# DeltaNet and a maxout FFN on one core: the last prologue links and the first four FFN pieces in program order, and a reordered second group

## The chip, the cores and the metric

The kernel runs on one core of a Trainium2 chip. The metric is the device time of one launch in microseconds (us). A core has five engines with queues of their own: TensorE (PE, with its weight loads PEld), VectorE (DVE), ScalarE (ACT), GpSimd (POOL) and SyncE (SP), which here only issues DMA transfers.

## The reference

There are two stages. The first is a delta-rule recurrence over 768 steps for 4 batches x 8 heads with head size 48, the second a maxout FFN over 3072 tokens.

```python
B, H, S, D = q.shape                       # 4, 8, 768, 48
k_n = k / (np.linalg.norm(k, axis=-1, keepdims=True) + 1e-06)
for t in range(S):
    y[:, :, t] = np.einsum('bhd,bhde->bhe', q[:, :, t], state)
    v_old = np.einsum('bhde,bhd->bhe', state, kt)
    state = state + bt[:, :, :, None] * np.einsum('bhd,bhe->bhde', kt, vt - v_old)

x = y.transpose(0, 2, 1, 3).reshape(B * S, H * D)          # (3072, 384)
h = np.maximum(np.maximum(x @ w1, x @ w2), x @ w3)         # 768 columns
out = h @ w_out                                            # (3072, 384)
```

All is float32. The FFN weights arrive as 64-bit numbers and are put together from their two halves on the chip.

## The kernel before

The sequence is cut into 12 chunks of 64 steps. A chunk has two units (two of the four batches each), so there are 24 units, and two chunks make a group: six groups, and a group's 512 tokens are also what one call of `ffn` takes. Within a chunk the steps depend on one another through a triangular system, which is solved first: `gram` multiplies keys with keys (tile `at`) and with queries (tile `pt`), `to_dram` and `blocks` bring the diagonal blocks of `at` into another layout through DRAM, and `solve(m)` substitutes for the two chunks of group m on DVE, column by column (L519 multiplies, L523 subtracts). For the first two groups (`FINE = 2`) the blocks have 16 columns, and `halves_z` and `halves_u` join two of them to one of 32 (tiles p_e, p_f). `join_z` and `join_u` (p_z, p_j) join the blocks of 32 to the full system `ut`, with T1, the transposed first block, from `turn_t1` (L569, L571). `old_k` and `old_q` read the state (p_k, p_q), `new` makes the update u (p_u), `step` adds it to the state `st` (p_s, L732), `to_y` makes the output (p_y) and `to_x` turns it into the FFN's input `xt` (p_x).

`ffn(m)` is a generator: each piece is one product with one of the three weights (p_h, three 128x128 blocks) and a copy on ACT or a maximum on DVE (L831, L833), and it ends with four pieces for the output (p_o). For m = 0, pieces 0 to 8 take the first 256 tokens and pieces 9 to 17 the other 256, for half of the hidden columns; so the first FFN can start when only chunk 0 is done. p_h and p_o share two PSUM buffers (`ps_ffn`), all products of the recurrence share three (`ps_two`).

Between two pieces the kernel writes the links of the next group. A table gives, for each piece, letters with a chunk or unit: z and j are the joins, e and f the halves, d is T1, k, q, u, s, y, x the recurrence, t and g the turns and Grams of a unit, L and N loads of keys and queries in blocks for a later turn. The loop of group 0 takes the links of group 1 from `EARLY_LINKS`, and also what is left of chunk 1 from `FIRST` (there T and P are the turns and Grams of queries alone). The loops of groups 1 to 4 use `LINKS` for the group after.

In the prologue and in the loops of groups 1 to 5, all engines follow the program (`manual_schedule()`). In the loop of group 0, only TensorE does; a planner puts the work of DVE, ACT, POOL and SP in the order that its own costs give.

The FFN weights come in 24 pieces of 384 KB through five buffers (`fetch`, L192). `some(conv, 1)` puts one of them together: ACT L211 and L220, POOL L215, DVE L230 and L234, POOL L238; a piece's DVE part is written one step after its ACT part, and each of its two temporary tiles has two buffers. `solve(1)` keeps its two tiles in the space of `wo_sb`, which the last six weight pieces fill later.

In the loops from group 1 on, `turn` is `turn_blocks`: DVE transposes (L385) from tiles `turned`, which `load_blocks` fills with eight key loads on SP and eight query loads on POOL (L369).

Of the kernel before, what the change touches and what calls it, by code (L numbers as in the profile page):

```python
# [21 lines left out]
def kernel(  # L22
# [31 lines left out]
    nc = tc.nc  # L54
# [70 lines left out]
    def load_q(n, queues=one_queue):  # L125
        load(q, qpad[n % NQ], n, queues)
# [61 lines left out]
    def fetch(queue=nc.scalar):  # L188
        if fetched[0] < len(pieces):
            _, src, (a, b) = pieces[fetched[0]]  # L190
            st = work.tile([128, 2 * 384], U32, name="w_bits", bufs=5)
            queue.dma_start(  # L192
                out=st.rearrange("p (a b) -> p a b", a=a), in_=src
            )
            staged.append(st)
            fetched[0] += 1
# [133 lines left out]
    def turn(n, parts=(0, 1), copy=nc.scalar.copy):  # L330

        if n not in kqts:
            kqts[n] = work.tile([128, NP, 2, 2, C], FP32, name="kqt", bufs=6)
        kqt = kqts[n]
        p_t = ps_two("p_t")
        for i in parts:
            src = (kpad[n % NK], qpad[n % NQ])[i]
            for j in range(NP):
                nc.tensor.transpose(
                    p_t[:, i, j * 128 : (j + 1) * 128],  # L340
                    src[:, 2 * j : 2 * j + 2],
                    ident,
                )
        some = slice(parts[0], parts[-1] + 1)
        copy(  # L345
            kqt.rearrange("p j b i t -> p i (j b) t")[:, some],
            p_t.rearrange("p i (x t) -> p i x t", t=C)[:, some],
        )
# [51 lines left out]
    def gram(n, parts=(0, 1), queues=one_queue, copy=nc.scalar.copy, later=False):  # L400
        kqt, g = kqts[n], n % 2
        p_g = ps_two("p_g")

        whole = len(parts) == 2 and not g
        for j in range(NP):
            for par in range(2):
                for bb in range(2):
                    kq = kqt[dims(par), j, bb ^ g]
                    for i in (0,) if whole else parts:
                        c0 = j * 128 + i * C  # L410
                        nc.tensor.matmul(  # L411
                            p_g[
                                rows(bb ^ (g * i)), par, c0 : c0 + C * (1 + whole)
                            ],
                            kq[:, 0],
                            kq if whole else kq[:, i],
                        )
        p_v = p_g.rearrange("p two (j i t) -> p two j i t", j=NP, i=2)
        if 1 in parts:
            pt = pts[n] = square("pt")  # L420
            if later:
                copy(by_par(pt), p_v[:, :, :, 1])
            else:
                masked(pt, p_v[:, :, :, 1])
        if 0 not in parts:
            return
        at = ats[n] = square("at")
        copy(by_par(at), p_v[:, :, :, 0])  # L428
        if queues:
            to_dram(n, queues)  # L430

    def to_dram(n, queues=one_queue):


        m, cc, g, at = n // 4, n % 4 // 2, n % 2, ats[n]
        if m not in at_d:
            at_d[m] = dram.tile([2, C, B, H, C], FP32, name="at_d")
        for bb in range(2):
            queues[bb].dma_start(
                out=at_d[m][cc, :, 2 * bb + g].rearrange("j h i -> j (h i)"),  # L440
                in_=at[rows(bb)].rearrange("p h i -> p (h i)"),
            )
# [123 lines left out]
    def turn_t1(c):  # L566

        t, u_t = t1[c % NU], ut[c % NU]
        nc.vector.transpose(out=t[:, 0], in_=u_t[:, 0, :, 0:BL])  # L569
        for bb in range(2):  # L570
            nc.vector.transpose(  # L571
                out=t[block(1 - bb), 1], in_=u_t[block(bb), 1, :, 0:BL]
            )
# [28 lines left out]
    def halves_z(c):  # L602
        if c not in fine:
            halves_t(c)
        at = [ats[2 * c + g] for g in range(2)]
        second = ut[c % NU].rearrange("p g h (f two x) -> p g h f two x", two=2, x=HB)
        for hs, p_v, copy in heads_of(c, "p_e", BL):
            for i, h in enumerate(hs):
                for bb, g in TILES:
                    r = rows(bb)  # L610
                    nc.tensor.matmul(
                        p_v[rows(bb ^ g), g, i], at[g][r, h], second[r, g, h, :, 1]
                    )
            copy(zs[c % NU][:, :, span(hs)], p_v)
# [7 lines left out]
    def halves_u(c):  # L622
        t, z = fine.pop(c), zs[c % NU]
        for hs, p_v, _ in heads_of(c, "p_f", BL):
            for i, h in enumerate(hs):
                for bb, g in TILES:
                    r = rows(bb ^ g)
                    nc.tensor.matmul(p_v[rows(bb), g, i], t[g][r, h], z[r, g, h])
            for f in (0, 1):
                for bb in range(2):  # L630
                    r = block(bb, f, HB)
                    negated(
                        bb,
                        ut[c % NU][r, :, span(hs), BL * f + HB : BL * (f + 1)],
                        p_v[r, :, :, HB * f : HB * (f + 1)],
                    )
        turn_t1(c)

    def join_z(c):
        at = [ats.pop(2 * c + g) for g in range(2)]  # L640
# [109 lines left out]
    def to_x(c):  # L750
        m, cc = divmod(c, 2)
        if m not in xts:
            xts[m] = work.tile([128, KT, TOK], FP32, name="xt")
        y_f = yts.pop(c).rearrange("p g h d -> p g (h d)")
        p_x = ps_two("p_x")
        for g in range(2):
            for t in range(KT):
                nc.tensor.transpose(
                    p_x[:, g, t * 128 : (t + 1) * 128],
                    y_f[:, g, t::KT],  # L760
                    ident,
                )
        xt = xts[m][:, :, cc * 256 : (cc + 1) * 256].rearrange(
            "p t (g x) -> p g t x", g=2
        )
        copied(c, xt, p_x[:, :, 0 : KT * 128].rearrange("p g (t x) -> p g t x", t=KT))
# [96 lines left out]
    def some(gen, n):  # L863
        for _ in range(n):
            if next(gen, gen) is gen:
                break
# [56 lines left out]
        masked(pts[n], by_par(pts[n]))  # L923
    for c in range(2):
        scale(c, nrm_0[:, c])
    some(conv, 2)
    for n in range(2):
        fetch(nc.sync)
    to_dram(6)
    to_dram(7)  # L930
    halves_z(0)
    some(conv, 1)
    fetch(nc.sync)
    blocks(1)
    halves_u(0)
    fetch(nc.sync)
    join_z(0)
    some(conv, 1)
    fetch(nc.sync)
# [7 lines left out]
    fetch(nc.sync)  # L947
    load_q(2)
    to_y(0)
    halves_z(1)  # L950
    some(conv, 1)
    fetch(nc.sync)
    to_x(0)
    load_q(3)
    load_q(4)
    load_v(2)
    some(conv, 1)
    fetch(nc.sync)
    solving = solve(1)
    by_hand.close()  # L960
    tc.no_sync_barrier()

    LINKS = {
# [4 lines left out]
    }  # L971
    EARLY_LINKS = {
# [3 lines left out]
    }  # L976

    FIRST = {
        0: "f1 s0 T2", 1: "z1 k1 P2 T3", 2: "j1", 3: "P3 q1", 4: "u1 T4",
        5: "y1", 6: "s1 T5 P4", 7: "x1 T6", 8: "P5 T7", 12: "P6", 14: "P7",  # L980
    }


# [3 lines left out]
    )  # L987
    MADE = dict(V=load_v, p=prep_sums, P=prep_values)
    UNIT = dict(t=turn, g=gram, K=load_k, L=load_blocks)
    OF_KEYS = dict(T=lambda n: turn(n, (1,)), P=lambda n: gram(n, (1,)))  # L990

    def links(m, names):
        for name in names.split():
# [18 lines left out]
                load_q(n + 3)  # L1012


    by_hand = ExitStack()
    by_hand.enter_context(tc.manual_schedule(engines={mybir.EngineType.PE}))
    for i, _ in enumerate(ffn(0)):
        if i > 2:
            some(conv, 1)
            fetch(nc.sync)  # L1020
        queries(FIRST.get(i, ""))
        links(1, EARLY_LINKS.get(i, ""))
        if 2 <= i < 9:
            some(solving, 3)
        if i == 4:
            load_v(3)
        if 5 <= i < 9:
            load_k(3 + i)
        if i in (8, 9):
            prep(i - 6)  # L1030
        if i == 12:
            load_q(11)
        if i in (15, 18):
            load_v(4 + i // 18)
        if i in (18, 20):
            prep(4 + i // 20)
        if i == 19:
            blocks(2)
        if i == 21:
            solving = solve(2)  # L1040
            some(solving, 1)
        if 21 <= i < 29:
            some(solving, 4)
        if i in (27, 28):
            load_blocks(i - 15)
# [52 lines left out]
```

## Time and profile before

| | us |
|---|---|
| median of 6 runs | 592.57 (590.66 to 595.69) |
| profiled execution | 590.66 |
| its span | 588.9 |
| PE busy | 538.7 (91%) |
| DVE busy | 343.7 (58%) |
| ACT busy | 140.4 (24%) |
| POOL busy | 119.8 (20%) |
| p_h, 702 matmuls (L823) | 301.6, mean 575 ns |
| p_o, 288 matmuls (L847) | 94.6, mean 487 ns |

The page also gives the span in 40 equal slices of 14.7 us, the busy share in tenths:

```
PE   5468468987999999999989999999999999999997
DVE  1658969388399363699653799663997432201110
PEclk9555859999999999999999999999999999999999
```

PEclk is the clock that TensorE was granted, in tenths of its full speed. The first FFN piece starts at 61 us, right after p_x of chunk 0. A line of an order in time has start, length, engine, line, operation and tiles; in brackets stand the time for which the engine had been idle and what ended it. "issue" is idle time for which the profile shows no reason.

### The profile page before, as it was taken

The numbers are of one execution on the slowest core, as the hardware profiler recorded it, in microseconds if no ns is written. First come the engines' busy times: TensorE is split into PE (matmuls) and PEld (weight loads), VectorE is DVE, ScalarE is ACT, GpSimd is POOL, SyncE is SP. The second block draws the span as 40 slices with busy tenths as digits, with TensorE's granted clock in tenths as the row PEclk, the third lists the DMA queues.
The fourth block names the chain that finished last, engine by engine and source line by source line (L and its number), as shares of the span: only waits on it lengthen the run. The fifth ranks groups of instructions, "written<-read, shape, count | busy, mean of one in ns | idle before, by whom it ended". The sixth has DMA issues, their size and how long they took to land.

```text
span 588.9 us, 18726 instructions
## 1 busy us (share of the span) xinstructions
PE 538.7 (91%) x8106; PEld 317.3 (54%) x8106; DVE 343.7 (58%) x778; ACT 140.4 (24%) x274; POOL 119.8 (20%) x209
## 2 busy tenths in 40 slices
PE   5468468987999999999989999999999999999997
PEld 5337356775555555555545555555455455554444
DVE  1658969388399363699653799663997432201110
ACT  3336635345211212111121121221211111010000
POOL 6024534127400243001913003800001000000000
PEclk9555859999999999999999999999999999999999
DMA  9998974655611563264664464843743102210002
GB/s 156 155 178 233 205 137 132 109 159 122 116 30 24 110 139 85 58 138 106 162 135 89 92 100 105 197 97 69 122 106 75 30 2 55 68 40 1 0 0 53
DMA packets 159505, 58.76 MB, mean 100 GB/s; under 512 B 141184, under 2 KB 153280, under 8 KB 159424
## 3 DMA queue, kind: packets, MB, share of 16 engines
q1 hardware_dynamic: 150736, 51.58, 42.2%
q0 software_dynamic: 3200, 4.82, 3.6%
q10 hardware_dynamic: 5488, 1.18, 1.2%
q8 instruction: 63, 1.03, 0.7%
q14 instruction: 18, 0.15, 0.1%
HBM read 40.21 MB, written 17.30 MB: 98 GB/s over the span
## 4 chain that ended last, share of the span: by engine, by line
PE 69%; DVE 13%; DMA 7%; SPq 4%; issue 3%; ACT 2%; POOL 1%; ACTq 0%; DVEq 0%; POOLq 0%
PE p_h L823 41%; PE p_o L847 13%; PE p_g L411 3%; DMA kpad<-in_k_dram 3%; PE p_k L676 2%; PE p_y L744 2%; DVE tmp L519 2%; PE p_u L704 2%; DMA y_d<-y_bl 1%; PE p_s L726 1%; SPq L369 1%; PE p_q L676 1%; DVE mant L234 1%; DVE y_bl L523 1%; PE p_j L659 1%
## 5 line engine op out<-in xcount | busy, mean ns | idle before, releaser
L823 PE MATMUL p_h<-xt,w_sb 128*128 128x512 f32 (+1 forms) x702 | 301.6, 575 | 1.4 <-DVE xt L809 1.4
L823 PEld LDWEIGHTS p_h<-xt,w_sb 128*128 128x128 f32 x702 | 128.7, 192 | 123.1 <-issue 113.4
L833 DVE TENSOR_TENSOR h<-h,p_h 128x512 f32<-128x512 f32 (+1 forms) x78 | 50.2, 644 | 103.3 <-PE p_h L823 103.1
L847 PE MATMUL p_o<-wo_sb,h 128*128 128x384 f32 x288 | 94.6, 487 | 0.0
L847 PEld LDWEIGHTS p_o<-wo_sb,h 128*128 128x128 f32 x288 | 54.2, 190 | 37.2 <-issue 1.0
L277 POOL TENSOR_TENSOR v_t<-v_t,nrm 128x768 f32<-128x768 f32 x12 | 17.7, 1478 | 197.4 <-DVE nrm L250 120.4
L523 DVE TENSOR_TENSOR y_bl<-y_bl,tmp 128x31 f32<-128x31 f32 (+20 forms) x139 | 53.4, 384 | 4.6
L369 POOL DMA_DIRECT2D turned<-in_q_dram x96 | 52.2, 551 | 3.9 <-POOL turned L364 3.1
L519 DVE TENSOR_TENSOR tmp<-x_bl,y_bl 128x31 f32<-128x31 f32 (+20 forms) x139 | 47.1, 339 | 4.0
L411 PE MATMUL p_g<-kqt 48*64 48x64 f32 (+1 forms) x1280 | 33.4, 250 | 13.7 <-ACT kqt L345 5.7
L831 ACT COPY h<-p_h 128x512 f32<-128x512 f32 (+1 forms) x39 | 21.5, 552 | 96.8 <-PE p_h L823 96.7
L411 PEld LDWEIGHTS p_g<-kqt 48*64 48x64 f32 x1280 | 28.0, 148 | 22.9 <-issue 10.6
L855 ACT COPY o_sb<-p_o 128x384 f32<-128x384 f32 x24 | 11.5, 478 | 81.4 <-PE p_o L847 73.7
L428 ACT COPY at<-p_g 128x512 f32<-128x512 f32 x21 | 12.3, 585 | 46.5 <-DVE pt L395 38.0
L238 POOL TENSOR_TENSOR w_sb<-mant,up 128x384 int32<-128x384 int32 x18 | 18.5, 1028 | 17.1 <-DVE mant L234 14.6
L732 DVE TENSOR_TENSOR st<-st,p_s 128x768 f32<-128x768 f32 x11 | 10.4, 950 | 17.5 <-PE p_s L726 17.5
L215 POOL TENSOR_SCALAR mant<-mant 128x384 f32<-128x384 f32 x24 | 13.0, 540 | 36.3 <-ACT mant L211 36.2
L385 DVE STREAM_TRANSPOSE kqt<-turned 128x256 f32<-128x256 f32 x48 | 17.3, 416 | 5.2 <-DMA turned<-in_k_dram 5.1
L688 DVE TENSOR_TENSOR v_t<-v_t,p_k 128x768 f32<-128x768 f32 x11 | 10.5, 952 | 16.9 <-PE p_k L676 16.9
L696 ACT COPY qs<-p_q 128x768 f32<-128x768 f32 x11 | 8.8, 798 | 47.8 <-DVE v_t L688 27.6
L676 PEld LDWEIGHTS p_k<-st,kqt 48*64 48x64 f32 x704 | 12.2, 142 | 11.9 <-issue 11.9
L395 DVE TENSOR_TENSOR pt<-p_g,mask 128x512 f32<-128x512 f32 x22 | 15.1, 688 | 6.0 <-PE p_g L411 5.7
(111 smaller groups left out, 495.0 us busy)
## 6 DMA issues: line engine op xcount, KB each, us to landing
w_bits<-in_moe_w_dram SPq DMA_DIRECT2D x18, 384.0 KB
at_d<-at SPq DMA_DIRECT2D x45, 128.0 KB
v_t<-in_v_dram SPq DMA_DIRECT2D x24, 192.0 KB
turned<-in_q_dram POOLq DMA_DIRECT2D x96, 48.0 KB, 3.1
turned<-in_k_dram SPq DMA_DIRECT2D x96, 48.0 KB
out_dram<-o_sb SPq DMA_DIRECT2D x48, 96.0 KB
kpad<-in_k_dram SPq DMA_DIRECT2D x44, 96.0 KB
y_x<-y SPq DMA_DIRECT2D x16, 192.0 KB
```

Of the source, the lines that this page charges most:

```text
L238: nc.gpsimd.tensor_tensor(out=dst.bitcast(I32), in0=mant_v.bitcast(I32), in1=up_v, op=ALU.add)
L277: nc.gpsimd.tensor_tensor(out=vts[c], in0=vts[c], in1=nrm[:, :, :, None].to_broadcast([128, 2, H, D]), op=ALU.mult,)
L369: (nc.sync, nc.gpsimd)[i].dma_start(out=t[p0 : p0 + 32, bb, at : at + NP * 2 * D].rearrange("p (j x) -> p j x", j=NP), in_=(k, q)[i][2 * b ...
L385: nc.vector.transpose(out=kqts[n][:, :, bb ^ (n % 2), i].rearrange("p j (r tb) -> p j tb r", tb=2), in_=t[:, bb, 32 : 32 + NP * 2 * D].rea ...
L411: nc.tensor.matmul(p_g[rows(bb ^ (g * i)), par, c0 : c0 + C * (1 + whole)], kq[:, 0], kq if whole else kq[:, i],)
L519: nc.vector.tensor_tensor(out=t_v, in0=row.to_broadcast(t_v.shape), in1=column.to_broadcast(t_v.shape), op=ALU.mult,)
L523: nc.vector.tensor_tensor(out=rest, in0=rest, in1=t_v, op=ALU.subtract)
L676: nc.tensor.matmul(p_b[rows(bb), par, c0 : c0 + D], kqt[g][dims(par), j, bb ^ g, i], st[dims(par), bb ^ g, g, j],)
L823: nc.tensor.matmul(p_h, w_sb[i][:, t, f * 128 : (f + 1) * 128], xt[:, t, lo : lo + w], start=(t == 0), stop=(t == KT - 1),)
L831: nc.scalar.copy(h, p_h)
L833: nc.vector.tensor_tensor(out=h, in0=h, in1=p_h, op=ALU.max)
L847: nc.tensor.matmul(p_o, hs[f][:, i * 128 : (i + 1) * 128], wo_sb[:, f], start=(f == 0), stop=(f == FT - 1),)
```

## The change

Five things are changed.

- The prologue in program order now goes on to piece 3 of the first FFN; the planner's part starts at piece 4. Four pieces and their links are therefore written out on all engines. A `some(conv, ...)` and `fetch` go with each piece from 4 on (before: from 3 on); the two weight steps behind solve(0) become one, and there is one more ahead of the loop, so eight stand ahead of it, as before.
- solve(1) is placed by hand: two steps at the end of the prologue, eleven behind the links of pieces 0 to 3 (letter S in `FIRST`), two behind each of pieces 4 to 7. Before, three steps stood behind each of pieces 2 to 8.
- `turn_t1` is called by itself and not at the end of `halves_u`: for chunk 0 in the prologue, for chunk 1 behind z1 of piece 1, for the second group one link after its halves.
- `EARLY_LINKS`: the halves of the second group start at piece 10 (before 12), its joins at 14 (before 16), and the rest of its recurrence one to three pieces earlier.
- `LINKS`, used by the loops of groups 1 to 4: d0 d1 and t2 change places (pieces 2 and 3).

No work is added or taken out: the matmuls, the weight steps, the steps of the substitution and the transfers are the same in number.

```diff
@@ halves_u
-        turn_t1(c)
@@ prologue
-    some(conv, 2)
+    some(conv, 1)
...
     to_dram(7)
+    halves_t(0)
     halves_z(0)
     some(conv, 1)
     fetch(nc.sync)
     blocks(1)
     halves_u(0)
-    fetch(nc.sync)
+    turn_t1(0)
     join_z(0)
...
     to_y(0)
-    halves_z(1)
     some(conv, 1)
     fetch(nc.sync)
+    halves_z(1)
+    load_q(3)
     to_x(0)
-    load_q(3)
+    for n in range(2):
+        some(conv, 1)
+        fetch(nc.sync)
     load_q(4)
     load_v(2)
-    some(conv, 1)
-    fetch(nc.sync)
     solving = solve(1)
-    by_hand.close()
-    tc.no_sync_barrier()
+    some(solving, 2)
@@ LINKS
-        0: "k0 q0 t0 L2", 1: "g0 t1 L3", 2: "g1 d0 d1", 3: "t2", 4: "z0", 5: "z1 g2",
+        0: "k0 q0 t0 L2", 1: "g0 t1 L3", 2: "g1 t2", 3: "d0 d1", 4: "z0", 5: "z1 g2",
@@ EARLY_LINKS
-        9: "k0 q0", 10: "t0", 11: "t1 g0", 12: "e0", 13: "e1 g1", 14: "f0 t2",
-        15: "f1 g2", 16: "z0 t3", 17: "z1 g3", 18: "j0", 19: "j1 u0", 20: "s0",
-        21: "k1 q1", 23: "u1 y0", 25: "s1", 26: "x0", 27: "y1", 29: "x1",
+        9: "k0 q0", 10: "e0 t0", 11: "e1 t1", 12: "f0 g0", 13: "f1 d0 g1",
+        14: "z0 d1 t2", 15: "z1 g2", 16: "j0 t3", 17: "j1 g3", 18: "u0", 19: "s0",
+        20: "k1 q1", 21: "y0", 22: "u1", 23: "x0", 24: "s1", 26: "y1", 28: "x1",
@@ FIRST
-        0: "f1 s0 T2", 1: "z1 k1 P2 T3", 2: "j1", 3: "P3 q1", 4: "u1 T4",
-        5: "y1", 6: "s1 T5 P4", 7: "x1 T6", 8: "P5 T7", 12: "P6", 14: "P7",
+        0: "f1 s0 T2 S1 S1", 1: "z1 d1 S1 k1 P2 T3 S1 S1", 2: "j1 S1 S1 S1",
+        3: "P3 S1 q1 S1 S1", 4: "u1 T4", 5: "y1", 6: "s1 T5 P4", 7: "x1 T6",
+        8: "P5 T7", 12: "P6", 14: "P7",
@@ OF_KEYS
+    S=lambda n: some(solving, n)
@@ loop of ffn(0)
-    by_hand = ExitStack()
-    by_hand.enter_context(tc.manual_schedule(engines={mybir.EngineType.PE}))
     for i, _ in enumerate(ffn(0)):
-        if i > 2:
+        if i == 4:
+            by_hand.close()
+            tc.no_sync_barrier()
+            by_hand = ExitStack()
+            by_hand.enter_context(tc.manual_schedule(engines={mybir.EngineType.PE}))
+        if i > 3:
             some(conv, 1)
             fetch(nc.sync)
         queries(FIRST.get(i, ""))
         links(1, EARLY_LINKS.get(i, ""))
-        if 2 <= i < 9:
-            some(solving, 3)
+        if 4 <= i < 8:
+            some(solving, 2)
```

More of the change, by code (lines that the diff above doesn't have):

```diff
@@ L989 @@
     UNIT = dict(t=turn, g=gram, K=load_k, L=load_blocks)
-    OF_KEYS = dict(T=lambda n: turn(n, (1,)), P=lambda n: gram(n, (1,)))
+    OF_KEYS = dict(S=lambda n: some(solving, n), T=lambda n: turn(n, (1,)), P=lambda n: gram(n, (1,)))
     def links(m, names):
```

## The prediction

> **What bounds the kernel now.** I read the busy time by stretch first, then TensorE's waits, then the order of time at the two places that the change touches. From 145 us to the end TensorE is never idle for long (80.00 of 80.00 us busy from 200 to 280, 78.35 from 280 to 360), so a microsecond that TensorE loses anywhere moves the end by one. Before 145 us it loses many:
>
> ```profile
> 60.00:70.00 10.00, 5.43 (x144) 4.46 (x144) 9.26 (x19) 5.53 (x14) 5.92 (x8) 0.99 0.96 185
> 70.00:80.00 10.00, 3.02 (x126) 2.79 (x127) 7.89 (x20) 4.97 (x12) 4.53 (x6) 0.50 1.19 204
> 80.00:90.00 10.00, 9.56 (x212) 7.77 (x212) 7.37 (x20) 4.86 (x11) 3.44 (x5) 0.66 0.54 125
> ```
>
> The columns are length, busy PE, PEld, DVE, ACT, POOL, then PE's granted clock, DMA share, GB/s: from 60 to 80 us TensorE works 8.45 of 20 us while DVE is nearly full, and its clock halves. Who it waited for, from 56 to 146 us (total, times, longest):
>
> ```profile
> PE p_z L646 <- DVE ut L618: 6.4, 1, 6.4
> PE p_k L676 <- issue: 4.1, 1, 4.1
> PE p_g L411 <- DVE z L650: 2.1, 1, 2.1
> PE p_g L411 <- DVE y L746: 1.9, 1, 1.9
> ```
>
> and the first two in order of time:
>
> ```profile
> 62.57 1.14 PE L628 MATMUL p_f<-z,t 64*64 64x32 f32 x64
> ...
> 65.08 1.46 PE L823 MATMUL p_h<-xt,w_sb 128*128 128x256 f32 x6
> 72.92 1.08 PE L646 MATMUL p_z<-ut,at 32*32 32x32 f32 x64 [6.38 <-DVE ut L618]
> 74.36 1.95 PE L676 MATMUL p_k<-st,kqt 48*64 48x48 f32 x62 [0.37 <-DVE st L732]
> 80.44 0.24 PE L676 MATMUL p_k<-st,kqt 48*64 48x48 f32 x1 [4.13 <-issue]
> ```
>
> p_f is done at 63.7, but DVE reaches its copy L618 only at 71.06, because the planner put eight weight instructions (L230, L234) and two reductions among the start of solve(1) and ahead of L618. The second place is the third FFN group, where DVE is in program order:
>
> ```profile
> 295.30 0.45 DVE L569 STREAM_TRANSPOSE t<-ut 128x256 f32<-128x256 f32 x1 [2.71 <-DMA ut<-y_d]
> ...
> 297.50 0.88 DVE L571 STREAM_TRANSPOSE t<-ut 32x256 f32<-32x256 f32 x2
> 300.86 0.45 DVE L385 STREAM_TRANSPOSE kqt<-turned 128x256 f32<-128x256 f32 x1 [2.48 <-DMA turned<-in_k_dram]
> 302.06 1.10 DVE L385 STREAM_TRANSPOSE kqt<-turned 128x256 f32<-128x256 f32 x3 [0.76 <-DMA turned<-in_k_dram]
> 303.08 0.65 DVE L833 TENSOR_TENSOR h<-h,p_h 128x512 f32<-128x512 f32 x1
> ```
>
> T1's six transposes fill a gap in which DVE would otherwise wait for the keys.
>
> **Part 1: four pieces in program order.** TensorE's order stays the same up to piece 10; DVE, ACT and POOL change. Nothing is added or removed; each engine's work is moved. Prologue: one weight step less ahead of join 0 takes 0.4 us off DVE's start (L583 follows the transfer that lands at 43.1 instead of an L234 that ends at 43.6); xt comes some 0.3 us earlier.
>
> (a) The way to L618. The reader of solve(1), ACT's L245, now stands behind the eighth weight step, whose L211 waits for POOL's L238 of the sixth: from the rows of 56 to 63 us I get L238 at 61.9 to 62.9, L211 and L220 to 63.9, L245 to 64.2. Then solve(1)'s start on DVE, undisturbed in solve(0): L246 at 22.50 to the end of the first L519/L523 pair at 25.88, 3.4 us, so 67.6. L618, ACT's L620, L618 take 0.42 + 0.40 + 0.45 = 1.3 us: 68.9. A clash with POOL as at 66.06 (L249 0.98 instead of 0.19) is 0.8 us; I take half. p_z starts at about 69.3 instead of 72.92: 3.6 gained (bounds 2.5 and 4.5). T1's three transposes (1.3 us) now come after st L732, so st ends at 70.2 and p_k starts at 70.25 instead of 74.36: 4.1 gained in all. Late next would be T1 for p_j, at about 73.5, but p_j comes behind p_h, at 76: covered.
>
> (b) The gap of 4.13 us in the middle of p_k. TensorE waits for nothing that the page knows; it ends at 80.44, just as the DMA share falls from 1.19 (76 to 80) to 0.07 (80 to 84). The page lists a queue "instruction" with 63 packets and 1.03 MB, 16 KB each; I read the gap as such a packet behind data. By about 74 us the changed order has issued six weight tiles, four query and one value load where before had nine, four, two and a key load: 3.5 against 5.2 MB, so the queue should drain near 70 to 72 us, about when p_k needs it. Bounds 0 and 4.13; I leave 1.0: 3.1 gained.
>
> The Trainium skill ("Runtime: NRT & Kernel Launch", Instruction fetch mechanics) says that the sequencer refills 16 KiB blocks by its own DMA queue and that crossing a block is mostly hidden. The 4.13 us here is not hidden; by the page the gap after the change would be 0 and the total 1.0 us lower.
>
> (c) The clock. With 6.38 and 4.13 us idle, p_k, p_g, p_t, p_h, p_j, p_h took 1.95 + 1.46 + 1.11 + 2.76 + 1.08 + 1.86 = 10.2 us; the same later, at full clock, take 1.15 + 0.69 + 0.65 + 1.56 + 0.75 + 1.46 = 6.3. 2.8 us of idling stay, and 2.15 us at 141 were enough to make the next p_h 4.54 instead of 2.84. I take half, 2.0 (bounds 0 and 3.9).
>
> (d) New waits. ACT's copy of u (L709) now stands behind the weight step of piece 9, whose L211 waits for POOL's L238 of piece 7, and that for its L234 on DVE, now put behind twelve L519/L523 pairs: p_y would wait 2.1 us against 0.83: 1.3 lost (bounds 0 and 3). Queued behind ACT's wait are u, the corners L714 and a kqt copy. Later, a kqt copy (L345) stands behind two further weight steps and holds p_x by 2.3 us, against 1.90 + 0.80 before (y and st late): 0.4 gained. SP: a query load that waits for p_t of piece 1 is now ahead of the next value and weight loads, up to 74 us; the five staged tiles cover it.
>
> **Part 2: links.** The substitution ends at about 88 us instead of 99.9, so y_d is issued some 10 us earlier, ahead of it on SP only loads that were issued by then; ut is there for joins from piece 10. Between 105 and 145 us before lost 0.32 + 0.63 + 0.46 + 0.61 + 0.35 + 1.13 + 2.15 = 5.65 us idle and 1.70 by the clock, 7.35. The same matmuls now stand in other order, with more between f and z. A new cost: ksum's loads for the norm of chunk 2 stand behind eight ut, three key and two query loads on SP; v_t L277 and L688 come late and p_k keeps one of three PSUM buffers: 1.2 us at t2. I estimate 4.7 left of 7.35: 2.6 gained (bounds 0 and 5).
>
> Early sum: 4.1 + 3.1 + 2.0 - 1.3 + 0.4 + 2.6 = 10.9, say 11 gained.
>
> **Part 3: T1 a link apart in the later groups.** t2's transposes (L385) now come ahead of T1's. In the group at 279 us they still wait for keys whose loads stand on SP behind y_d and eight ut loads, so they end at 303.16 as before; T1's 0.45 + 0.88 + 0.45 + 0.88 = 2.66 us, with gaps 2.75, then delay L833 from 303.08 to 305.9. The FFN has two PSUM buffers, and the p_h that started at 304.24 needs the one that L833 frees: it starts at 306.6, 2.36 lost. In the group at 363 us t2 ends at 386.24, the p_h of 387.32 moves to 389.65: 2.33 lost. In the group at 197 us keys were there at 213.04 without a wait; the loads were issued by 207.7, and a row's median to landing is 3.1 us: at 210.3 it may wait up to 0.5. The group at 446 has no t2: nothing. Sum 4.7; for the clock after 1.65 + 2.36 us idle I add 1.0 (0, or 1.70 in each group, 3.4): 5.7 lost (bounds 0, if keys land sooner, and 8.5).
>
> By the skill ("TensorE: Matmul & The Clock Gate", Part 1) the clock halves only after an idle window of about 3.4 us; that would make this 4.7 instead of 5.7. The 2.15 us at 141 us, followed by a granted clock of 0.61 from 144 to 148, speak against it.
>
> **Sum.** -11 + 5.7 = -5.3 us. The profiled execution took 590.66 with a span of 588.9; it is the fastest of six, 1.9 under their median of 592.57. So 583.6 for the span, 587.3 for the median. 0.5%, 3.0 us, is about what a measurement can tell from no change.
>
> **Rivals.**
> - T1 costs nothing: if t2's keys land some 3 us earlier, only the early gain is left: 592.57 - 11 = 581.6. For: SP starts these loads right behind y_d and ut, so anything that brings y_d forward does it. Against: nothing in the later groups' order on SP changes. 0.20.
> - Gain and loss cancel: the gap of 4.13 us stays, as TensorE reaches the same instruction while loads are in flight; (c) falls with it: 11 - 3.1 - 2.0 = 6 against 5.7: 592. For: DMA share is 1.04 already at 64 to 68 us. 0.18.
> - Slower: DVE, in program order, is stopped by t2 in all three groups. If the keys are late by 1 us more in each, and the clock falls by (c)'s 1.70 in the last two, 1 + 2 x (2.35 + 1 + 1.70) = 11.1 are lost; it decides once the early gain is under 8.1, where the loss is over 3 us; with 6 it is 597.7. For: DVE already waits 2.48 and 0.98 us for these keys. Against: no load is moved. 0.17.
>
> The forecast has 0.45. Faster: 0.45 + 0.20 less a tail = 0.64; within 0.5%: 0.18 + a little = 0.19; slower 0.17. The likeliest case's own range is 583 to 591; the range of 580 to 596 takes in the first rival's middle and the edge of the last.
>
> **What would show it.** (a) p_z near 69 us and its wait for L618 under 3.5 us. (b) No issue gap over 2 us in p_k. (c) Granted clock above 0.5 from 70 to 80 us. (d) p_y waiting for ACT's u. Part 2: p_h of 512 columns first at about 135 instead of 144 us. Part 3: L569 right behind L385 in the groups at about 270 and 355 us, and p_h there waiting 2 us or more for L833. If p_z still waits 6 us, or TensorE's idle time before 145 us is no shorter, the forecast is wrong.

## The result, and the profile after

The changed kernel takes 598.18 us (median of 19 runs, 595.20 to 601.37), the kernel before 592.96 beside it (median of 40, one of which took 2975 us). The ratio is 1.009, with a 95% interval of 1.0067 to 1.0112: 5.3 us slower. The forecast was 587.3, faster. The profiled execution took 599.14 us with a span of 597.2, against 590.66 and 588.9.

The busy time by stretch of the changed kernel, the same three stretches as before (columns as there: length, busy PE, PEld, DVE, ACT, POOL, PE's granted clock, DMA share, GB/s) and two later ones:

```profile
60.00:70.00 10.00, 8.80 (x142) 7.46 (x143) 8.19 (x20) 3.77 (x10) 3.00 (x4) 0.50 1.06 202
70.00:80.00 10.00, 8.17 (x233) 6.46 (x234) 7.49 (x19) 1.16 (x2) 0.00 (x0) 0.67 0.34 54
80.00:90.00 10.00, 7.94 (x206) 6.39 (x194) 8.62 (x25) 4.62 (x9) 2.39 (x4) 0.97 0.16 37
...
280.00:360.00 80.00, 75.89 (x1196) 41.00 (x1189) 50.49 (x115) 14.42 (x28) 17.27 (x37) 0.96 0.54 111
360.00:430.00 70.00, 66.38 (x1072) 35.59 (x1071) 42.46 (x97) 12.03 (x22) 16.80 (x32) 0.95 0.50 109
```

The two later stretches in the kernel before:

```profile
280.00:360.00 80.00, 78.35 (x1233) 42.75 (x1232) 54.97 (x124) 15.03 (x30) 20.90 (x42) 1.00 0.55 116
360.00:430.00 70.00, 69.66 (x1148) 37.15 (x1150) 47.96 (x110) 13.34 (x24) 15.32 (x31) 1.00 0.57 118
```

From 60 to 80 us TensorE is now busy 16.97 us instead of 8.45, but much of that is the same work at half clock (0.50 to 70 us). From 280 us on it is idle 4.1 and 3.6 us, where the kernel before was idle 1.65 and 0.34, and its clock, 1.00 before, is 0.96 and 0.95. The first two places in order of time on TensorE, and what stood at the same place in the FFN group at 280 us:

```profile
61.20 2.90 PE L822 MATMUL p_h<-xt,w_sb 128*128 128x256 f32 x6 [2.79 <-POOL mant L215]
...
70.81 0.75 PE L645 MATMUL p_z<-ut,at 32*32 32x32 f32 x64
71.49 1.14 PE L675 MATMUL p_k<-st,kqt 48*64 48x48 f32 x62
74.46 0.24 PE L675 MATMUL p_k<-st,kqt 48*64 48x48 f32 x1 [1.83 <-issue]
...
90.18 1.48 PE L743 MATMUL p_y<-u,pt 64*64 64x48 f32 x64 [2.24 <-ACT u L708]
...
300.62 1.33 PE L411 MATMUL p_g<-kqt 48*64 48x128 f32 x32 [1.91 <-DVE kqt L385]
304.15 5.36 PE L822 MATMUL p_h<-xt,w_sb 128*128 128x512 f32 x6 [2.20 <-DVE h L832]
```

The last two lines in the kernel before:

```profile
302.98 1.33 PE L411 MATMUL p_g<-kqt 48*64 48x128 f32 x32 [1.65 <-DVE kqt L385]
304.24 2.84 PE L823 MATMUL p_h<-xt,w_sb 128*128 128x512 f32 x6
```

p_z no longer waits 6.38 us, and the gap in p_k is 1.83 instead of 4.13 us. Against that, p_y waits 2.24 us as forecast, and at 304 us a new wait of 2.20 us is followed by a p_h of 5.36 us, 2.84 before. The 2.79 us that p_h waits at 61 us are no loss of the change. The page names POOL's L215, which writes nothing that p_h reads; what p_h needs is xt (the traces of e4 and e9 name it), whose copy L808 ends at 61.05. In the kernel before the same copy ends at 60.96 and p_h starts at 61.11: there the wait was 1.37 us only because p_x ended later. DVE in that group, in order of time:

```profile
299.70 1.10 DVE L385 STREAM_TRANSPOSE kqt<-turned 128x256 f32<-128x256 f32 x3 [2.50 <-DMA turned<-in_k_dram]
300.72 0.41 DVE L569 STREAM_TRANSPOSE t<-ut 128x256 f32<-128x256 f32 x1
301.14 0.88 DVE L571 STREAM_TRANSPOSE t<-ut 32x256 f32<-32x256 f32 x2
302.03 0.45 DVE L569 STREAM_TRANSPOSE t<-ut 128x256 f32<-128x256 f32 x1
302.49 0.88 DVE L571 STREAM_TRANSPOSE t<-ut 32x256 f32<-32x256 f32 x2
303.40 0.69 DVE L832 TENSOR_TENSOR h<-h,p_h 128x512 f32<-128x512 f32 x1
```

T1 (L569, L571) fills no gap any more; it lies whole between the last key transpose and the maximum L832 that frees p_h's buffer.

Because TensorE's order of work is known, the starts of a few matmuls show where time is won and lost. This table puts the profiled execution of every kernel of the study side by side (us; "gap" is the idle time put down to issue inside the p_k at 70 to 80 us; the last four columns are the first p_k of the later FFN groups, called the first to fourth group below; e1 and so on are the experiments):

| kernel | p_z | gap | p_x | first | second | third | fourth |
|---|---|---|---|---|---|---|---|
| before | 72.92 | 4.13 | 104.49 | 199.85 | 282.04 | 366.24 | 449.25 |
| e2, before + swap | 72.56 | 2.4 | 103.22 | 198.54 | 280.77 | 369.77 | 458.19 |
| e11, before + later t2 | 72.38 | 2.1 | 103.96 | 196.74 | 278.92 | 361.27 | 444.19 |
| changed | 70.81 | 1.83 | 98.89 | 197.20 | 279.41 | 368.62 | 457.52 |
| e1, swap undone | 70.20 | 1.5 | 98.22 | 196.54 | 278.85 | 364.81 | 448.49 |
| e4, T1 behind the maximum | 70.13 | 1.1 | 98.74 | 196.81 | 278.98 | 365.04 | 450.48 |
| e3, first part alone | 70.41 | 2.0 | 98.67 | 199.86 | 282.04 | 367.82 | 451.22 |
| e5, e1 + sums first | 70.65 | 1.3 | 94.55 | 193.33 | 275.53 | 359.47 | 442.79 |
| e6, e3 + sums first | 71.33 | 1.2 | 96.43 | 199.72 | 281.90 | 368.34 | 451.87 |
| e7, e5 + later t2 | 70.39 | 1.4 | 95.50 | 195.89 | 278.10 | 360.64 | 443.55 |
| e8, e5 + later loads | 70.52 | 0 | 94.51 | 191.09 | 273.26 | 359.53 | 442.76 |
| e9, e7 and e8 | 69.68 | 1.5 | 95.03 | 194.21 | 276.39 | 358.68 | 440.86 |
| e10, e9 + five pieces | 70.42 | 1.7 | 95.91 | 203.42 | 285.60 | 367.80 | 452.90 |

Up to 190 us the first three rows are the same program. They differ by 3.1 us at the first group, and in gap by 2.0: that is how far one profiled execution can be trusted there. The profiled executions of e5 and e11 were also 2.9 and 3.1 us faster than the medians of their kernels, that of e7 2.0 slower. The changed kernel is 5.6 us ahead of before at p_x, 2.6 ahead at the second group, and then loses 5.0 in the second group (89.21 against 84.20) and 5.9 in the third (88.90 against 83.01).

### The profile page after: what moved, and what is told of

Same layout as the page of the kernel before. It is cut to its first block, busy times and chain, and to the rows that moved or that the text cites. A ratio compares the mean times of both kernels' runs of the same rounds, so it can differ in the third digit from the quotient of the medians.

```text
span 597.2 us, 18730 instructions
## 1 busy us (share of the span) xinstructions
PE 548.8 (92%) x8106; PEld 321.9 (54%) x8106; DVE 343.1 (57%) x778; ACT 139.8 (23%) x274; POOL 119.9 (20%) x209
## 3 DMA queue, kind: packets, MB, share of 16 engines
q8 instruction: 63, 1.03, 0.7%
## 4 chain that ended last, share of the span: by engine, by line
PE 69%; DVE 4%; SPq 2%; issue 1%; DMA 1%; ACT 0%; POOL 0%; DVEq 0%; POOLq 0%; ACTq 0%
PE p_h L822 42%; PE p_o L846 16%; PE p_g L411 2%; PE p_u L703 2%; PE p_y L743 2%; PE p_k L675 2%; PE p_s L725 1%; PE p_q L675 1%; SPq L369 1%; PE p_j L658 1%; DMA turned<-in_k_dram 1%; DVE tmp L519 1%; DVE y_bl L523 1%; SPq L537 0%; DVE h L832 0%
## 5 line engine op out<-in xcount | busy, mean ns | idle before, releaser
L822 PE MATMUL p_h<-xt,w_sb 128*128 128x512 f32 (+1 forms) x702 | 311.0, 590 | 7.2 <-DVE h L832 4.4
L822 PEld LDWEIGHTS p_h<-xt,w_sb 128*128 128x128 f32 x702 | 133.4, 199 | 131.6 <-issue 114.7
L832 DVE TENSOR_TENSOR h<-h,p_h 128x512 f32<-128x512 f32 (+1 forms) x78 | 50.3, 645 | 101.6 <-PE p_h L822 101.3
L385 DVE STREAM_TRANSPOSE kqt<-turned 128x256 f32<-128x256 f32 x48 | 17.5, 417 | 18.8 <-DMA turned<-in_k_dram 18.6
L215 POOL TENSOR_SCALAR mant<-mant 128x384 f32<-128x384 f32 x24 | 12.8, 535 | 42.7 <-ACT mant L211 42.6
L743 PEld LDWEIGHTS p_y<-u,pt 64*64 64x64 f32 x768 | 13.4, 144 | 10.5 <-issue 7.6
L618 DVE TENSOR_SCALAR ut<-p_j 32x512 f32<-32x512 f32 (+1 forms) x13 | 8.3, 647 | 17.4 <-ACT ut L620 17.3
L703 PEld LDWEIGHTS p_u<-v_t,ut 64*64 64x64 f32 x768 | 13.4, 142 | 8.4 <-issue 7.8
```

Source lines behind the costliest of these rows:

```text
L703: nc.tensor.matmul(p_v[rows(bb ^ g), g, i], ut[c % NU][rows(bb), g, h], rhs[rows(bb), g, h],)
L743: nc.tensor.matmul(p_v[rows(bb), g, i], pt[g][r, h], u[r, g, h])
L822: nc.tensor.matmul(p_h, w_sb[i][:, t, f * 128 : (f + 1) * 128], xt[:, t, lo : lo + w], start=(t == 0), stop=(t == KT - 1),)
L832: nc.vector.tensor_tensor(out=h, in0=h, in1=p_h, op=ALU.max)
```

## The experiments

The theory going in: the time is lost by T1 behind t2 in the second and third groups (the swap of d0 d1 and t2 in `LINKS`), and the early part, all the rest of the change, gains some 2.6 us. The main rival: the early part itself makes the later groups late.

**e1: the changed kernel with the swap undone.**

```diff
-        2: "g1 t2", 3: "d0 d1", 4: "z0", 5: "z1 g2",
+        2: "g1 d0 d1", 3: "t2", 4: "z0", 5: "z1 g2",
```

> The changed kernel with T1 (d0 d1) back ahead of t2 in the later groups; everything early as changed. Theory (the loss is made by T1 behind t2, in the groups m=2 and m=3): the first p_k of group m=2 starts some 2.6 us earlier than in the kernel before, and nothing is lost from there on, so 592.9 - 2.6, about 590, 0.4 to 0.5% faster than before; the first p_h after t2 takes 2.8 us and doesn't wait for L832. Rival (the early part itself makes the later groups late, through ut, y_d or the queues): 2.2 us of waiting or a p_h of over 4 us stay in m=2 or m=3, and the time is 594 or more.

590.11 us, ratio to before 0.9953 (0.9930 to 0.9977): 2.8 us faster. The theory's time. But one of its signs failed: the p_h after t2 doesn't always take 2.84 us, also without the swap.

```profile
299.92 1.33 PE L411 MATMUL p_g<-kqt 48*64 48x128 f32 x32 [1.78 <-DVE kqt L385]
301.18 4.54 PE L822 MATMUL p_h<-xt,w_sb 128*128 128x512 f32 x6
```

There is no wait for L832, yet behind 1.78 us of waiting for the keys the p_h took 4.54 us, 1.70 more than at full clock (granted 0.65 from 300 to 304 us). In the profiled execution of before, 1.65 us of waiting had no such effect.

**e2: the kernel before with the swap alone.**

```diff
-        2: "g1 d0 d1", 3: "t2", 4: "z0", 5: "z1 g2",
+        2: "g1 t2", 3: "d0 d1", 4: "z0", 5: "z1 g2",
```

> The kernel before with the swap in LINKS alone (t2 ahead of d0 d1). Theory: groups m=2 and m=3 lose some 5 us each: 2.2 to 2.4 us of p_h waiting for the maximum L833, and 2.3 to 2.5 us because that p_h runs at half clock, 5.2 to 5.4 us instead of 2.84. In all 592.9 + 10.9 = 604, 1.8% slower. If only the idle time counts and the clock hardly, as in my forecast, +5.7: 598.7. Rival (the loss needs the early change): within 1.5 us of 593.

599.52 us, ratio 1.0109 (1.0083 to 1.0135): 6.5 us lost, between the theory's 10.9 and the forecast's 5.7. So the loss needs nothing of the early part. The waits in the trace are 2.19 and 2.20 us for L833, and both p_h behind them take 5.49 us; its groups take 89.00 and 88.42 us, as in the changed kernel. The first of them:

```profile
305.18 5.49 PE L823 MATMUL p_h<-xt,w_sb 128*128 128x512 f32 x6 [2.19 <-DVE h L833]
```

That the medians differ by less than these traces may have its reason in e1: the kernel before, with the same groups, can lose the 1.70 us too, and its profiled execution didn't.

**e3: the first four pieces in program order alone, both lists of links as before.**

```diff
-        9: "k0 q0", 10: "e0 t0", 11: "e1 t1", 12: "f0 g0", 13: "f1 d0 g1",
-        14: "z0 d1 t2", 15: "z1 g2", 16: "j0 t3", 17: "j1 g3", 18: "u0", 19: "s0",
-        20: "k1 q1", 21: "y0", 22: "u1", 23: "x0", 24: "s1", 26: "y1", 28: "x1",
+        9: "k0 q0", 10: "t0", 11: "t1 g0", 12: "e0", 13: "e1 g1", 14: "f0 d0 t2",
+        15: "f1 d1 g2", 16: "z0 t3", 17: "z1 g3", 18: "j0", 19: "j1 u0", 20: "s0",
+        21: "k1 q1", 23: "u1 y0", 25: "s1", 26: "x0", 27: "y1", 29: "x1",
```

> The changed kernel with both lists of links as before (T1 directly behind f0 and f1): only the first four pieces in program order are left of the change. Theory (Part 1 gives the 5.6 us that p_x shows in the changed kernel, and Part 2 gives back 3 of it): p_x near 98.9 us and a time of 587.5 to 589, below e1. Rival (Part 2 gained 2.6, as forecast, and Part 1 nothing in the end): the time is 592 to 593, 2 to 3 us over e1.

592.63 us, ratio 0.9984 (0.9959 to 1.0008): no gain. The rival was right: the new links are worth about what the forecast gave Part 2 (0.9953 / 0.9984 = 0.9969, 1.8 us, with intervals that overlap a little; 3.3 by the table's first group), and Part 1 ends at nothing, though it is 5 us ahead at p_x. TensorE in e3 shows where that goes:

```profile
121.15 0.69 PE L411 MATMUL p_g<-kqt 48*64 48x64 f32 x32
126.30 1.41 PE L628 MATMUL p_f<-z,t 64*64 64x32 f32 x64 [4.46 <-DVE v_t L687]
...
130.14 2.77 PE L822 MATMUL p_h<-xt,w_sb 128*128 128x256 f32 x6
```

L687 subtracts p_k from v_t and so frees one of p_k's PSUM buffers. It waited for v_t to be scaled by the norm of the keys, whose last step on DVE (L250) comes here at 123.37 and in the kernel before at 100.43. Up to 121 us e3 keeps its lead: the p_g at 121.15 comes 5.6 us earlier than in the kernel before. The p_h at 130.14 is 0.5 us ahead. The norm needs ksum, two small transfers on SP. In the kernel before and then in e3 they are issued at:

```profile
87.44 1.37 SPq L273 DMA_DIRECT2D ksum<-kflip  x2
```

```profile
97.06 4.83 SPq L537 DMA_DIRECT2D ut<-y_d  x8
...
111.04 2.15 SPq L273 DMA_DIRECT2D ksum<-kflip  x2
```

So ksum goes out 23.6 us later than before. Most of that is its source: DVE makes kflip (L268) at 91.04 instead of 69.61. By then the substitution, which ends 9 us earlier, is over, and on SP ksum stands behind y_d, eight ut loads, weight loads and the next keys and queries, for 19 us (17 before, behind other loads).

**e4: the changed kernel with T1 one link later, behind the maximum.**

```diff
-        2: "g1 t2", 3: "d0 d1", 4: "z0", 5: "z1 g2",
+        2: "g1 t2", 3: "", 4: "d0 d1 z0", 5: "z1 g2",
```

> The changed kernel with d0 d1 one link later (4 in place of 3), so that T1 stands behind the maximum of piece 4 and ahead of that of piece 5, still behind t2. Theory (T1 costs time only because it stands ahead of the maximum that frees the buffer of the next p_h but one): as e1 within 1.5 us, no p_h over 4 us. Rival (T1 anywhere behind t2 costs its 2.7 us on DVE, since the next maximum is late instead): p_h waits 2 us at the following maximum and the time stays near 598.

592.50 us, ratio 1.0003 (0.9976 to 1.0029). Between the two. No p_h waits for a maximum or takes over 2.84 us in these groups, as the theory has it:

```profile
299.98 1.33 PE L411 MATMUL p_g<-kqt 48*64 48x128 f32 x32 [1.70 <-DVE kqt L385]
301.24 2.84 PE L822 MATMUL p_h<-xt,w_sb 128*128 128x512 f32 x6
...
309.14 0.29 PE L411 MATMUL p_g<-kqt 48*64 48x64 f32 x2 [0.79 <-ACT ut L620]
309.70 1.48 PE L411 MATMUL p_g<-kqt 48*64 48x64 f32 x62 [0.26 <-DVE kqt L385]
```

But DVE is late for what follows, and the next p_g waits 1.05 us (1.03 in the third group). So of the changed kernel's loss the place ahead of the maximum is about two thirds (1.009 - 1.0003 of 1.009 - 0.9953); the rest stays as long as T1 is behind t2.

**e5: e1 with the key sums four pieces earlier.**

```diff
-        if i in (8, 9):
-            prep(i - 6)
+        if i in (4, 5):
+            prep(i - 2)
```

> The first of these experiments (changed kernel with d0 d1 back ahead of t2) plus one edit: the key sums of chunks 2 and 3 (prep) are made four pieces earlier, at pieces 4 and 5 in place of 8 and 9, so that their ksum loads go out on SP ahead of the substitution's ut and the next key loads. Theory (the early gain of 4.5 to 6 us seen at p_x is eaten at 125 us, because the norm of chunk 2 comes at 123 us in place of 100 and v_t L687 keeps a PSUM buffer): the norm is done by 100 us, p_t no longer waits 1.66 us for v_t L687, the half-clock p_t and p_h behind it go, and p_k of group m=2 starts 2 to 3.5 us earlier than 278.85: 587, 1.0% under the kernel before. Rival (it is ACT and POOL with the weights that hold the links, and v_t is only the last in time): the wait moves to kqt, at or z, and the time stays within 1 us of 590.

587.04 us, ratio 0.9922 (0.9886 to 0.9958), the theory's time, though its interval overlaps that of e1. kflip is made at 86.90, only 4 us earlier than in e3, but ksum is issued at 88.60, ahead of y_d. The last step of the norm (L250) comes at 99.90, no matmul waits for L687 any more, and the second group starts at 275.53 instead of 278.85. But the traces don't lay the gain at that wait alone. The first line is the wait in e1, the other two are new in e5:

```profile
126.94 0.97 PE L339 MATMUL p_t<-ident,kpad 128*128 128x128 f32 x4 [1.66 <-DVE v_t L687]
```

```profile
103.07 1.15 PE L675 MATMUL p_q<-st,kqt 48*64 48x48 f32 x64 [1.76 <-DVE pt L395]
121.58 1.98 PE L411 MATMUL p_g<-kqt 48*64 48x64 f32 x60 [1.93 <-issue]
```

e5 is already 3.7 us ahead of e1 at p_x (94.55 and 98.22), before the wait in question, and loses all of it behind the two new ones: its p_z comes at 127.41, in e1 at 124.52. It is ahead again only from 139 us, where e1's p_g waits 1.74 us for kqt and e5's doesn't wait. That the edit gains some 3 us is measured (3.1 by the medians); that the norm is the reason is not shown by it.

**e6: the same edit on e3.**

> The kernel with only the first four pieces in program order (both lists of links as before; it measured 592.63, no gain) plus the same earlier sums. Theory: its wait of 4.46 us of p_f for v_t L687 and the 2.4 us of half clock behind it go, so that p_z, 136.72 there and 137.23 before the change, comes at 131 to 133 and the time falls by 4 to 6 us to 587 to 589. Rival: p_z stays at 136 or later and the time at 592.

594.10 us, ratio 1.0042 (1.0011 to 1.0072). The theory fell here. The norm's L250 comes at 101.80 and the 4.46 us are gone, but p_z comes at 135.26, and the second group at 281.90, as in e3. What took its place:

```profile
113.04 0.63 PE L339 MATMUL p_t<-ident,qpad 128*128 128x128 f32 x4 [1.15 <-DMA qpad<-in_q_dram]
...
122.95 1.27 PE L411 MATMUL p_g<-kqt 48*64 48x64 f32 x59 [2.49 <-issue]
124.16 2.93 PE L822 MATMUL p_h<-xt,w_sb 128*128 128x256 f32 x6
...
138.15 0.63 PE L339 MATMUL p_t<-ident,kpad 128*128 128x128 f32 x4 [2.14 <-DVE ut L618]
```

With the old links, where e, f and z follow one another closely, the time won is lost to a query load, an issue gap with a p_h of 2.93 us behind it, and DVE's L618 behind a weight step; at 105 us p_q also waits 1.77 us for pt (L395), as in e5. So the late norm is one taker of Part 1's gain in e3, and not the only thing that can take it. The medians of e6 and e3 lie 1.5 us apart, which the spread of their runs hardly separates.

**e7: e5 with t2 and its g2 one link later in the later groups.** The maximum of piece 4 is then ahead of t2 on DVE, and g2 a piece behind it.

```diff
-        2: "g1 d0 d1", 3: "t2", 4: "z0", 5: "z1 g2",
-        6: "j0 t3",
+        2: "g1 d0 d1", 3: "", 4: "t2 z0", 5: "z1",
+        6: "g2 j0 t3",
```

> e5_sums_first with t2 one link later and its g2 one link later in the groups m=1 to m=3 (3: nothing, 4: t2 z0, 5: z1, 6: g2 j0 t3): the maximum of piece 4 is then ahead of t2 on DVE. Theory (what costs time in the later groups is DVE stopped in program order by keys that land late, and the clock that falls after TensorE's wait): the waits of p_g for kqt L385 (1.8 and 1.0 us) go, no p_h of 4.5 us is left, and 2.7 to 4.4 us are gained over e5: some 583.5, 1.5% under before. Rival (the wait goes wherever t2 goes): p_h or p_j waits 1 us or more in both groups and the time is within 1 us of e5.

582.98 us, ratio 0.9844 (0.9795 to 0.9894), as the theory has it. DVE still waits 2.65 us for the keys, but no matmul does:

```profile
297.33 2.84 PE L822 MATMUL p_h<-xt,w_sb 128*128 128x512 f32 x6
300.10 1.10 PE L411 MATMUL p_g<-kqt 48*64 48x128 f32 x32
301.13 0.75 PE L658 MATMUL p_j<-z,t 32*32 32x32 f32 x64
```

**e8: e5 with two of the prologue's weight loads later.**

```diff
-    for n in range(2):
-        some(conv, 1)
-        fetch(nc.sync)
+    some(conv, 1)
+    some(conv, 1)
...
         queries(FIRST.get(i, ""))
+        if i in (2, 3):
+            fetch(nc.sync)
```

> e5_sums_first with the last two weight loads of the prologue (384 KB each) issued at pieces 2 and 3, so that some 4 us less of transfers lie ahead of p_k. Theory (the 'issue' gap in p_k, 1.1 to 2.0 us in the changed kernels and 2.4 to 4.1 before, is an instruction transfer behind data): the DMA share falls before 72 us and the gap is under 0.7 us. Rival (a fixed cost of the place in the program): the gap stays between 1.1 and 2.0 us.

The gap in p_k is gone, and the DMA share from 64 to 72 us is much lower. In e5, and then in e8:

```profile
64.00:68.00 4.00, 4.00 (x132) 3.91 (x125) 3.56 (x11) 0.76 (x3) 0.96 (x2) 0.50 0.97 234
68.00:72.00 4.00, 4.00 (x116) 3.19 (x118) 3.13 (x9) 1.46 (x3) 0.00 (x0) 0.71 0.83 120
```

```profile
64.00:68.00 4.00, 4.00 (x131) 3.91 (x132) 3.42 (x10) 0.93 (x5) 1.13 (x2) 0.50 0.64 113
68.00:72.00 4.00, 4.00 (x125) 3.33 (x127) 3.28 (x11) 1.53 (x3) 0.00 (x0) 0.76 0.27 49
```

In this execution the gap is gone and the load is lower, as the theory has it; e9 speaks against it. For the time it does little: p_y waits 2.42 us for u (2.1 in e5), p_x comes at 94.51 against 94.55, and 585.97 us (ratio 0.9906, 0.9871 to 0.9941) can't be told from e5.

**e9: e7 and e8 together.**

> e7_keys_behind_max and e8_fetch_later together: first four pieces in program order, new early links, earlier sums, the last two prologue weight loads at pieces 2 and 3, t2 behind the maximum of piece 4. Theory (early and late gains add, as nothing late in the kernel depends on the early milliseconds but the start): p_k of group m=2 near 274 to 276, no wait for kqt L385 in the later groups, 581.5 to 583, 1.6 to 1.9% under before. Rival (e8's early gain was a matter of one execution): within 1 us of e7's 583.

582.16 us, ratio 0.9830 (0.9792 to 0.9868): 1.7% faster than before, the lowest median of the study. It can't be told from e7. The gap is back in its profile with 1.52 us, though the loads are moved and the DMA share is as low as in e8 (0.68 from 64 to 68 us, 0.29 from 68 to 72). So a low DMA share does not by itself remove the gap, and its cause stays open. The second and third groups take 82.29 and 82.18 us.

**e10: e9 with piece 4 in program order too, its weight step behind u1.** The end of the hand-written order moves from piece 4 to piece 5, and prep from pieces 4 and 5 to 5 and 6.

```diff
-        if i == 4:
+        if i == 5:
             by_hand.close()
...
-        if i > 3:
+        if i > 4:
             some(conv, 1)
             fetch(nc.sync)
         queries(FIRST.get(i, ""))
+        if i == 4:
+            some(conv, 1)
+            fetch(nc.sync)
```

> e9_both with piece 4 in program order too (five pieces in place of four), its weight step put behind u1, and prep one piece later: ACT's copy of u (L708) then stands ahead of the weight step whose L211 waits for POOL. Theory (step (d) of the forecast: p_y waits 2.1 to 2.4 us because u stands behind a weight step): that wait falls under 0.7 us and p_y comes 1.5 to 2 us earlier; of it 1 us reaches the end, 581 to 582. Rival (what is won at p_y is lost at the next wait, for st, at or a weight tile): p_y early, p_x and everything behind as in e9, the same time or up to 1.5 us more.

594.41 us, ratio 1.0032 (1.0004 to 1.0061): 12 us over e9. The wait for u is gone and p_y comes at 85.38 instead of 88.69, but of these 3.3 us nothing is left at p_x (95.91, in e9 95.03): a p_g at 92.68 waits 3.0 us for y. Behind p_x TensorE waits for pt (who waited for whom, 56 to 190 us: total, times, longest; the third line is the p_h at 61 us):

```profile
PE p_f L628 <- DVE pt L395: 3.1, 1, 3.1
PE p_g L411 <- DVE y L745: 3.0, 1, 3.0
PE p_h L822 <- POOL mant L215: 2.9, 1, 2.9
PE p_q L675 <- DVE pt L395: 2.6, 1, 2.6
```

From 90 to 100 us DVE is busy 9.84 of 10 us, against 8.80 in e9. From p_x to the first group e10 takes 107.5 us, e9 99.2. The rival was right up to p_x and too mild behind it; three things were moved at once, and which of them costs the most was not taken apart.

**e11: the kernel before with only t2 and g2 later** (the diff of e7).

> The kernel before with only t2 and g2 one link later in the later groups (3: nothing, 4: t2 z0, 5: z1, 6: g2 j0 t3), T1 where it was. Theory: the 1.65 and 0.34 us of p_g waiting for kqt L385 go, and with them the clock loss that follows the first in some executions (a p_h of 4.5 in place of 2.84 us): 2 to 3.7 us gained, 589 to 590.5. Rival (e7's gain over e5 needs the early change): 592 to 593.

588.71 us, ratio 0.9938 (0.9912 to 0.9964): 3.7 us gained without anything early. No matmul waits for L385 in the later groups; the second and third take 82.35 and 82.92 us, against 84.20 and 83.01. The rest of the lead that its table row shows stood already at the first group, where the program is that of before.

## Why the forecast was wrong

The forecast's net was 11 gained and 5.7 lost. Measured: 2.8 gained (e1) and 8.1 lost (changed kernel over e1, 1.009 / 0.9953). Both were wrong in the same direction. The greater error is the step "Early sum: ... say 11 gained", and in it the term of Part 2, "I estimate 4.7 left of 7.35: 2.6 gained": behind p_x, the output of chunk 1, time was lost and not gained. The smaller error is the term for the clock in Part 3.

- **(a)** p_z at 69.3 was forecast, 69.7 to 71.3 are seen. But the same matmul in three executions of the old order starts at 72.4 to 72.9, so 2.2 are gained (means of 72.6, and of 70.4 in the changed kernel, e1, e3 and e4) and not 3.6. For p_k, where the sum has 4.1, it is 3.1 (means of 74.4 and 71.3). The chain on DVE was right.
- **(b)** The gap: 3.1 were forecast by taking 4.13 to 1.0. The old order shows 4.13, 2.4 and 2.1, mean 2.9; the changed one (its own profile, e1, e3, e4) 1.83, 1.5, 2.0 and 1.1, mean 1.6. So 1.3. The reading of it as an instruction transfer behind data fits e8 and not e9; no run shows what the gap is.
- **(c)** The clock, 2.0: mostly not there. p_t, p_h, p_j, p_h behind the gap took 1.11 + 2.77 + 1.08 + 1.71 = 6.67 us, 6.81 before. All that the forecast added up to 10.2 us takes 9.3 on average in the changed kernel, e1, e3 and e4, and 9.6 in the three executions of the old order: 0.3 gained. In the changed kernel's profile the clock had fallen at 61 us already, but so it had in e2 and e11, where the early part is that of before (p_h there takes 2.90 us too). The slow matmuls from 61 to 70 us cost little: in e4, where p_f runs at full clock, p_z waits 3.6 us for L618 and starts at 70.13, 0.7 us ahead of the changed kernel's, which doesn't wait.
- **(d)** was right for p_y, which waits 2.24 us for u (2.1 forecast). p_x waits 0.67 for kqt where 2.3 were forecast (2.13 in e3), so this term was too high. And e10 shows that p_y's wait is a cover: without it the time goes elsewhere.
- Together (a) to (d) gave 8.3; seen at p_x are 5.3 (mean of 103.9 in the old order, 98.6 in the changed kernel, e1, e3 and e4).
- **Part 2** is the term that failed. As a difference between two lists of links it was right in size (1.8 from e1 and e3, against 2.6). But the sum took it as a gain on top of Part 1, and the 5.3 us at p_x end as 2.8 in e1. From p_x to the first group the old order takes 94.5 us (mean of three), the changed kernel, e1 and e4 98.2. The "4.7 left of 7.35" are 9.4 in e1: its waits from 118 to 141 us are 0.71 + 0.58 + 0.61 + 1.66 + 0.81 + 1.74 = 6.1 us, and slow matmuls behind two of them cost 3.3. Right in kind and wrong in size was the "new cost ... 1.2 us at t2": in e1 the wait is 1.66 us, and p_t, p_t, p_h behind it take 0.97 + 1.06 + 2.45 us instead of 0.66 + 0.60 + 1.46, 3.4 us in all. In e3 it is 4.46 us before any clock, and there it takes nearly the whole lead. Whether the gain would have stayed without it is open: in e6 it did not.
- **Part 3** was right about the place, the mechanism and the idle time: 2.20 and 2.20 us against 2.36 and 2.33, nothing in the first and the fourth group. Mis-sized was "for the clock ... I add 1.0": the p_h behind the waits take 5.36 and 5.18 us instead of 2.84, 4.9 in all. The bound given for it, 1.70 a group, was a p_h half slow; these are slow nearly from end to end. In the third group p_g also waited 1.40 us for the keys, 0.34 before; with 0.60 in e2 and 0.96 in e1 that wait seems to go with the execution and not with the swap.
- The slower rival came closest in time (597.7), by another way: it wanted DVE stopped in all three groups and the keys later. The keys were hardly later in the second group (p_g waits 1.91 us instead of 1.65), and the first lost nothing; that its figure is near is luck.

## What to carry to other kernels

A gain ahead of a planned stretch is not a gain until the stretch has been looked at again: here a small load (ksum), ready late, came to stand behind large ones on the shared queue, and e3 lost 4.46 us to it. Giving it an earlier place was not enough by itself in e6, where other waits took over. On an engine in program order, work that needs nothing late belongs in front of an instruction that waits for a transfer, and what frees a double-buffered matmul belongs in front of both: that alone gains 3.7 us in e11, and 4 to 5 in e7 over e5 (4.1 by the medians, 4.7 by 0.9844 / 0.9922, with wide intervals). And a wait taken from one profiled execution has a spread of its own: the means of three executions in place of the one would have cut steps (a) and (b) by 0.3 and 1.3 us.

## What was not expected of the hardware

TensorE's clock fell after short waits, and not always. After 1.78 us (e1) and 1.60 us (e3) of waiting the next p_h took 4.54 us; after 1.65 (before) and 1.70 us (e4) it took 2.84. In e10 it took 4.54 after a single wait of 0.64 us, at 396 us (granted clock 0.68 from 396 to 400), while 0.61 us in e3 and 0.98 in e4 had no effect. After two waits close together, 0.6 to 1.9 us, a p_g of 1.33 and 2.2 us more, it took 5.36 and 5.18 in the changed kernel and 5.49 both times in e2. The Trainium skill ("TensorE: Matmul & The Clock Gate", Part 1) describes a free-running window of about 3.4 us, and a fall to half clock after an idle window. A free-running window would fit the spread between executions, though no run here shows the window itself; the length doesn't fit, since the longest of these waits is 2.2 us, and the measurement decides.

TensorE's issue gap in p_k comes behind the same matmul, the 62nd of 64, in every profile but e8's, and differs by 2 us between executions of one program (4.13, 2.4, 2.1). Behind another such gap, of 2.49 us in e6, the p_h took 2.93 us instead of 1.56. With the DMA share equally low, the gap in p_k was absent in e8 and 1.52 us in e9.
